# A linear-attention and two-layer kernel: the start of the program is rewritten and the order of its first ten chunks is replaced

## The chip, the cores and the metric

The kernel runs on one core of one Trainium2 chip. The metric is the device time of one execution in microseconds (us): the median of the runs. A profile of one execution, taken by the hardware profiler, shows what each engine did: PE is TensorE, PEld its weight loads, DVE is VectorE, ACT is ScalarE, POOL is GpSimd, SP is SyncE, which here only issues transfers.

## What is computed

An attention with a decaying state (batch 4, 8 heads, 768 steps, head size 48), and then two matrix products with a leaky ReLU between them, on 3,072 tokens of 384 features and 2,048 hidden features:

```python
state = np.zeros((B, H, D, D), dtype=np.float32)
for t in range(S):
    kt, vt, rt = (k[:, :, t], v[:, :, t], r[:, :, t])
    cur = np.einsum('bhd,bhe->bhde', u[None] * kt, vt)
    y[:, :, t] = np.einsum('bhd,bhde->bhe', rt, state + cur)
    state = w[None, :, :, None] * state + np.einsum('bhd,bhe->bhde', kt, vt)
x = y.transpose(0, 2, 1, 3).reshape(B * S, H * D)
h = x @ w_in
out = np.maximum(0.01 * h, h) @ w_out
```

## The kernel before

The 3,072 tokens are cut into 24 chunks of 128, six for each batch entry. Inside a chunk the recurrence becomes matrix products: r is multiplied by a table of w to the power (t - 64), k by one of w to the power (63 - t), so that their product over the head size carries the decay; what lies at or above the diagonal is masked away, and the diagonal itself, which carries u, is added apart. A state of 48 by 48 for each head goes from chunk to chunk and is zero at the start of each batch entry.

The program is not written with loops that the engines run. `add` appends operations with the names they read and write, `Sched.resolve` (L75) turns these into semaphore waits, and each of the five engines then works through its own operations strictly in the order in which they were added. Transfers are in these streams too: SP issues r of chunk 0, the stores of the output and the transposing transfers; ACT issues k of chunk 0; POOL issues every other load, and each of these keeps it busy.

The order at the start is written by hand: the string LOADS gives the order in which POOL issues the loads (r3 is r of chunk 3, wi1 the second quarter of w_in, wo2 a quarter of w_out, id and tri the making of the identity and of the mask), and ORDER gives the order of the steps. A letter is a step and a number its chunk:

- P (`prep`, L303): on DVE, r and k times their tables into `qk`, two instructions; from chunk 8 on also the transposing transfer on SP that fills `tp`.
- T (`turn`, L342): for chunks 0 to 7 the same transposition by eight matmuls against the identity and two copies out of PSUM.
- A (`a_mm`, L369): eight matmuls, the products of all pairs of steps, in two PSUM banks. M (`a_mask`, L383): their masking into `at` on DVE, one instruction for each bank. From chunk 8 on the mask is copied onto a tile that POOL has filled with the diagonal.
- X (`diag`, L315): on DVE the product q*k of the transposed chunk, for the diagonal of chunks 0 to 7; K (`kv_mm`, L396): matmuls for the diagonal's sums and for the new state; Q (`prep2`, L320): v times these sums into `vs`; from chunk 8 on Q makes the sums on DVE with `u_tab` and POOL the diagonal tile (L342). S (`state`, L453): the state times its decay, on DVE.
- Y (`y_part`, L504, with `y_mm`, L466): the chunk's output, in matmuls of 32 columns of weights, four of them side by side, and a copy into `xT` on ACT.
- G (`g1`, L512): a quarter of the first product of one chunk, 12 matmuls of 128 columns, and the leaky ReLU on ACT; it needs that quarter of w_in. J (`g1_pair`, L530): an eighth of it for two chunks, 6 matmuls of 256 columns. H (`g2`, L548): the second product of a chunk, 16 matmuls of 384 columns, a copy on ACT and a store that SP issues; it needs all of w_out.
- C and W: the decay as columns (`decay_columns`, 16 small matmuls of the rows w and w*u) and as table. U: `u_tab`, u spread over all partitions by a matmul. F: matmuls on ones that compute nothing. L: the loads of a later chunk, held back until a given G or J has run.

What stands ahead of ORDER: w comes as a single row, a matmul against a row of ones (L287) spreads it over 128 partitions, ACT takes its logarithm (L289) and makes the two tables from it (L290, L291). POOL makes identity and mask with a select each (L255, L259); DVE fills the padding of v and qk with zeros (L278, L282). Eight PSUM banks are handed out in turn by `next_bank`.

After ORDER, from chunk pair 3 on, a loop (L576) repeats one pattern for each pair m: J for the pair, the steps Q, X, A, M of the pair after next, Y of the next pair, K, S, P two pairs on, and H of the pair before.

## Time and profile before

| | us |
|---|---|
| median of 3 runs | 173.33 (173.15 to 173.61) |
| span of the profiled execution | 171.8 |
| TensorE busy in it | 163.4 |
| VectorE, ScalarE, GpSimd busy | 95.7, 92.5, 102.7 |
| first matmul of T0 | 7.30 |
| first matmul of G0.0 | 14.08 |
| first matmul of an H | 42.59 |
| last copy out of PSUM | 168.94 |

The page gives the span of the profiled execution, from its first to its last instruction; its time with what lies around the span is not given, so the runs' median stands beside it. The DMA engines are in use until some 120 us:

```profile
DMA  5999999999999999999499499899008011011112
GB/s 98 119 150 157 171 153 173 200 179 144 112 98 240 94 145 126 202 101 116 133 93 138 128 89 143 147 116 217 0 4 214 4 46 46 4 46 50 46 48 92
```

The 40 digits are 40 equal slices of the span, 4.3 us each. A digit is the mean busy share of the core's 16 DMA engines in tenths; the row under it is what they moved. In a list of instructions the columns are the start, the length, the engine, the line, the operation, what it writes and reads, and in brackets the idle time of the engine before it and what ended that.

### The profile page before, as it was taken

To read this page: it belongs to the slowest core of one execution; us is meant where nothing else is said; L and a number is where in the kernel's file an instruction comes from. 1 tells how busy PE (TensorE), PEld (TensorE's weight loads), DVE (VectorE), ACT (ScalarE), POOL (GpSimd) and SP (SyncE) were. 2 spreads that over 40 slices of the span, in tenths; PEclk is the share of its full clock that TensorE was granted. 3 is DMA by queue.
4 is the path that set the end of the run, shared out by engine and by line. 5 is a ranking of instruction groups with operands and counts; after the bars stand their busy time and mean duration, and the time that the engine had idled before them with its cause. 6 is when DMAs were issued, how large, how long until landed. Compare 5 with 4: busy or idle time off the path is not lost.

```text
span 171.8 us, 5029 instructions
## 1 busy us (share of the span) xinstructions
PE 163.4 (95%) x2179; PEld 122.4 (71%) x2179; DVE 95.7 (56%) x209; ACT 92.5 (54%) x169; POOL 102.7 (60%) x117
## 2 busy tenths in 40 slices
PE   6799999969999989999999999999999999999993
PEld 1578799859666856876877867868868768678661
DVE  7699859550999679079189197296396520000000
ACT  4755698759123841942934934825817718539121
POOL 7999999990379998972993997957207200000000
PEclk9999999999999999999999999999999999999999
DMA  5999999999999999999499499899008011011112
GB/s 98 119 150 157 171 153 173 200 179 144 112 98 240 94 145 126 202 101 116 133 93 138 128 89 143 147 116 217 0 4 214 4 46 46 4 46 50 46 48 92
DMA packets 98970, 19.66 MB, mean 114 GB/s; under 512 B 92290, under 2 KB 98948, under 8 KB 98948
## 3 DMA queue, kind: packets, MB, share of 16 engines
q0 software_dynamic: 76512, 10.03, 89.7%
q1 hardware_dynamic: 21394, 9.11, 27.1%
q8 instruction: 17, 0.28, 0.7%
q10 hardware_dynamic: 1042, 0.20, 0.6%
q14 instruction: 5, 0.04, 0.1%
HBM read 20.45 MB, written 4.72 MB: 146 GB/s over the span
## 4 chain that ended last, share of the span: by engine, by line
PE 76%; DMA 9%; DVE 6%; POOL 6%; issue 2%; ACT 0%; POOLq 0%; ACTq 0%
PE ps L555 30%; PE ps L538 28%; PE ps L521 6%; PE ps L493 6%; DMA tp<-qk 5%; DMA w_in_sb<-in_moe_w_in_dram 4%; PE ps L377 3%; PE ps L408 2%; DVE qk L307 2%; POOL v_sb L210 2%; POOL r_sb L210 2%; POOL k_sb L210 2%; PE ps L355 1%; DVE ku L330 1%; DVE s_tok L334 1%
## 5 line engine op out<-in xcount | busy, mean ns | idle before, releaser
L555 PE MATMUL ps<-w_out_sb,gT 128*128 128x384 bf16 x384 | 64.5, 326 | 0.0
L538 PE MATMUL ps<-xT,w_in_sb 128*128 128x256 bf16 x480 | 54.5, 273 | 0.0
L555 PEld LDWEIGHTS ps<-w_out_sb,gT 128*128 128x128 bf16 x384 | 36.9, 98 | 23.4
L342 POOL TENSOR_TENSOR at<-ident,s_tok 128x512 bf16<-128x512 bf16 x32 | 33.8, 1081 | 30.3 <-DVE s_tok L334 30.3
L544 ACT ACTIVATE gT<-ps 128x512 bf16<-128x512 f32 x80 | 47.8, 597 | 7.0 <-PE ps L538 2.1
L538 PEld LDWEIGHTS ps<-xT,w_in_sb 128*128 128x128 bf16 x480 | 46.7, 98 | 6.4
L561 ACT ACTIVATE out_sb<-ps 128x384 f32<-128x384 f32 x24 | 11.8, 490 | 55.1 <-PE ps L555 55.1
L391 DVE CAST_PREDICATED at<-mask,ps 128x512 bf16<-128x512 uint16 x32 | 19.8, 684 | 27.6 <-PE ps L377 25.3
L210 POOL DMA_DIRECT2D v_sb<-in_v_dram x24 | 22.6, 948 | 0.4 <-issue 0.4
L210 POOL DMA_DIRECT2D k_sb<-in_k_dram x23 | 21.7, 945 | 0.0
L210 POOL DMA_DIRECT2D r_sb<-in_r_dram x23 | 21.4, 932 | 0.0
L508 ACT ACTIVATE xT<-ps 128x384 bf16<-128x384 f32 x24 | 11.0, 490 | 4.8 <-PE ps L493 4.3
L521 PE MATMUL ps<-xT,w_in_sb 128*128 128x128 bf16 x192 | 12.3, 219 | 0.3 <-DMA w_in_sb<-in_moe_w_in_dram 0.3
L493 PE MATMUL ps<-at,v_sb 128*32 128x128 bf16 x384 | 11.9, 224 | 0.0
L521 PEld LDWEIGHTS ps<-xT,w_in_sb 128*128 128x128 bf16 x192 | 11.1, 98 | 1.0 <-DMA w_in_sb<-in_moe_w_in_dram 0.6
L526 ACT ACTIVATE gT<-ps 128x512 bf16<-128x512 f32 x16 | 9.6, 599 | 3.6 <-PE ps L521 3.0
L332 DVE TENSOR_TENSOR rku<-r_sb,ku 128x384 bf16<-128x384 bf16 x16 | 10.8, 674 | 0.5
L387 DVE TENSOR_TENSOR at<-ps,mask 128x512 bf16<-128x512 f32 x16 | 10.3, 682 | 1.3 <-PE ps L377 1.3
L493 PEld LDWEIGHTS ps<-at,v_sb 128*32 128x32 bf16 x384 | 9.1, 98 | 2.0 <-issue 0.5
L366 ACT ACTIVATE tp<-ps 128x512 bf16<-128x512 f32 x15 | 8.2, 596 | 3.8 <-PE ps L355 3.8
L493 PE MATMUL ps<-tp,st 128*32 128x128 bf16 x240 | 10.1, 219 | 0.0
L377 PE MATMUL ps<-tp 48*128 48x128 bf16 x192 | 9.1, 228 | 0.9 <-DMA tp<-qk 0.7
(62 smaller groups left out, 134.5 us busy)
## 6 DMA issues: line engine op xcount, KB each, us to landing
out_dram<-out_sb SPq DMA_DIRECT2D x24, 192.0 KB, 2.2
v_sb<-in_v_dram POOLq DMA_DIRECT2D x24, 96.0 KB, 5.9
r_sb<-in_r_dram POOLq DMA_DIRECT2D x23, 96.0 KB, 5.1
k_sb<-in_k_dram POOLq DMA_DIRECT2D x23, 96.0 KB, 5.0
w_in_sb<-in_moe_w_in_dram POOLq DMA_DIRECT2D x4, 384.0 KB, 7.4
w_out_sb<-in_moe_w_out_dram POOLq DMA_DIRECT2D x4, 384.0 KB, 11.1
tp<-qk SPq DMA_TRANSPOSE x16, 3.4
r_f<-in_r_dram SPq DMA_DIRECT2D x1, 192.0 KB, 3.5
```

The costliest lines, as they stand in the source:

```text
L210: add("pool", lambda: G.dma_start(dst, src), R=pace, W=[(which, n)], dma=f"{which}{n}")
L332: add("dve", lambda: V.tensor_tensor(rku[i2][:, :], r_of(n), ku[i2][:, :], ALU.mult), R=[("r", n), ("ku", i2)], W=[("rku", i2)])
L342: add("pool", lambda hh=hh, s_of=s_of: G.tensor_tensor(at[ia][:, hh, :, :], ident[:, :].unsqueeze(1).to_broadcast([128, NP, 128]), s_of.un ...
L377: last = PE.matmul(at_bank[n][hh][0][:, 128 * p:128 * p + 128], tp[it][rows, NP + p, :], tp[it][rows, p, :], start=True, stop=True)
L391: add("dve", lambda hh=hh, part=part: V.copy_predicated(at[n % NAT][:, hh, :, :], mask[:, :].bitcast(mybir.dt.uint16).unsqueeze(1).to_broa ...
L493: last = PE.matmul(ps_y[32 * q:32 * q + 32, 128 * s:128 * s + 128], a, m, start=first_mm, stop=last_mm)
L508: add("act", lambda: A.activation(xT[m % NX][:, :, 128 * half:128 * half + 128], ps_y[:, 0:HD].rearrange("p (s t) -> p s t", t=128), AF.Copy),
L521: last = PE.matmul(ps_g[:, 128 * f:128 * f + 128], w_in_sb[:, s, 128 * fb:128 * fb + 128], xT[ix][:, s, t], start=s == 0, stop=s == NSL - 1)
L538: last = PE.matmul(ps_g[:, 256 * f:256 * f + 256], w_in_sb[:, s, 128 * fb:128 * fb + 128], xT[ix][:, s, :], start=s == 0, stop=s == NSL - 1)
L544: add("act", lambda: A.activation(gT[ig][:, 2 * j:2 * j + 2, :].rearrange("p f t -> p (f t)"), ps_g[:, :], AF.Prelu, alpha=0.01), R=[key], ...
L555: last = PE.matmul(ps_o[:, 0:HD], gT[ig][:, s, 128 * half:128 * half + 128], w_out_sb[:, s, :], start=s == 0, stop=s == NFB - 1)
L561: add("act", lambda: A.activation(out_sb[io][:, :], ps_o[:, 0:HD], AF.Copy), R=[key], W=[("o", io)])
```

## The change

`LOADS` is gone: the loads stand in ORDER as small letters among the steps, and ORDER is another one. As an engine's order is that of the string, a load's place among steps matters only against other work of POOL.

- w is loaded spread over 128 partitions by a transfer that reads the row 128 times, so the matmul that spread it is gone, and with it the two early fills. u comes the same way into `u_bc`, on SP, once chunk 1 has been turned (`u_table`). w and u also come as 8 rows of 48, and C multiplies these by a small selection matrix, four matmuls in place of 16; their product is step Z.
- One ramp (column minus partition) on POOL gives the exponents, the selection matrix, the identity and the mask, by comparisons on DVE.
- DVE clears the padding of qk 0 to 2 and v 0 to 2; `pad` on POOL clears the rest.
- r and k lie side by side in one tile; step B makes both products in one instruction (P still makes two), also in the loop. The transposing transfer is a step of its own, D.
- M takes both PSUM banks in one instruction. M1.2 lets ACT copy one of the two banks, M3.1 and M7.1 both, before DVE masks the copy. X7.1 puts X on POOL. Both copies of T0 go through ACT.
- Y of chunks 0 to 7 adds the diagonal by three matmuls of full width in place of twelve of 32 columns.
- The last H is cut into 256 and 128 columns, each with its own copy and store.

```diff
-FIRST, EARLY = 6, 2
-LOADS = """r1 k1 r2 k2 wi0 id v1 r3 tri k3 v2 wi1 k4 r4 v3 wi2 k5 r5 r6 k6 v4 v5 k7 wi3 r7 v6 v7 wo3 wo2 wo1 wo0"""
+FIRST = 6
 ORDER = """
-C W P0 P1 F1 T0 T1 P2 A0 X0 M0 A1 K0 T2 Q0 X1 Y0 A2 S0 M1 K1 X2 G0.0 Q1 P3 S1 Y1 T3 K2 M2 G1.0 X3 A3 U G0.1 S2 G1.1 Q2 M3 Y2 K3 P4
-T4 Q3 G2.0 G2.1 G0.2 S3 G2.2 G1.2 Y3 P5 A4 P6 X4 M4 T5 X5 G3.0 K4 Q4 A5 S4 T6 G3.1 K5 G3.2 Y4 M5 L8 Q5 Y5 P7 A6 G1.3 J2.0 J2.1 T7
-M6 X6 X7 K6 J2.2 J2.3 A7 S6 J2.4 J2.5 L9 Q6 G2.3 G0.3 J2.6 M7 L10 J2.7 L11 G3.3 K7 S7 P8 Q7 Q8 P9 H0 Q9 K8 H1 P10 L12 K9 H2 S8 S9
-Y6 Y7 A8 A9 P11 M8 H3 M9 L13
+r1 k1 v1 Z r2 k2 P0 r4 k3 C T0 A0 X0 P1 M0.0 v2 K0 r3 W T1 Q0 k4 A1 S0 pad wi0 X1 v3 B2 M1.2 Y0 K1 T2 Q1 k5 S1 P3 X2 r5 wi3 Y1 T3 K2 v4 v5 B4 wi1 v7 k6 r6 k7 Q2 T4 S2 X3.0 r7 v6 A2 wi2 A3 F2 M2.0 M3.1 G1.0 G0.0 K3 X4.0 Q3 B5 Y2 A4 Y3 S3 T5 G2.0 M4.0 G3.0 G0.3 K4 X5.0 G1.3 wo1 wo3 wo2 Q4 wo0 K5 Q5 G3.3 S4 L8 A5 M5.0 Y4 G1.1 G2.1 G2.3 L9 G3.1 P6 Y5 T6 G0.1 X6.0 J2.7 U J2.2 B7 J2.0 T7 L10 J2.4 J2.1 K6 G0.2 Q6 G2.2 X7.1 S6 J2.5 A7 A6 M6.0 M7.1 P8 G1.2 D8 J2.6 K7 G3.2 J2.3 Y6 B9 Q7 L11 H1 Q8 S7 K8 D9 S8 H2 H3 Q9 H0 Y7 L12 A8 A9 K9 B10 D10 B11 M8 M9.0 S9 D11 L13
...
-    def row(h):
-        return dram(h, 0, [[HD, 1], [1, HD]])
...
-    add("sp", lambda: SP.dma_start(w_row[:, :], row(w)), W=["w_row"], dma="w")
-    add("act", lambda: A.dma_start(u_row[:, :], row(u)), W=["u_row"], dma="u")
+    def spread(h):
...
+    add("sp", lambda: SP.dma_start(w_bc[:, :], spread(w)), W=["w_bc"], dma="w")
...
-    add("pool", lambda: G.iota(tcol[:, :], pattern=[[0, 1]], base=0, channel_multiplier=1,
-                               allow_small_or_imprecise_dtypes=True), W=["tcol"])
+    add("sp", lambda: SP.dma_start(w_h[:, :], w), W=["w_h"], dma="wh")
+    add("sp", lambda: SP.dma_start(u_h[:, :], u), W=["u_h"], dma="uh")
+    add("pool", lambda: G.iota(ramp[:, :], pattern=[[1, 128]], base=0, channel_multiplier=-1,
+                               allow_small_or_imprecise_dtypes=True), W=["ramp"])
     load_one(0, "v")
...
+    def load(name):
+        if name == "pad":
+            add("pool", lambda: G.memset(pad_v(3, NST), 0.0), W=[("v0", 1)])
+            add("pool", lambda: G.memset(qk_all[:, 3:NQK, :, D:E], 0.0), W=[("qk0", i) for i in range(3, NQK)])
...
+    add("dve", lambda: V.tensor_scalar(pick[:, :], ramp[0:H, 0:H], 0.0, None, ALU.is_equal), R=["ramp"], W=["pick"])
+    add("dve", lambda: V.tensor_scalar(ident[:, :], ramp[:, :], 0.0, None, ALU.is_equal), R=["ramp"], W=["ident"])
+    add("dve", lambda: V.tensor_scalar(mask[:, :], ramp[:, :], 1.0, None, ALU.is_ge), R=["ramp"], W=["mask"])
+    add("dve", lambda: V.memset(qk_all[:, 0:3, :, D:E], 0.0), W=[("qk0", i) for i in range(3)])
+    add("dve", lambda: V.memset(pad_v(0, 3), 0.0), W=[("v0", 0)])
+    add("dve", lambda: V.memset(wu[:, :, :], 0.0), W=["wu"])
...
-    fill(EARLY)
-    add("pe", lambda: PE.matmul(ps_w[:, 0:HD], one_row[:, :], w_row[:, :], start=True, stop=True),
-        R=["one_row", "w_row"], W=[key_w, "bc"])
-    add("act", lambda: A.activation(lnw[:, :], ps_w[:, 0:HD], AF.Ln), R=[key_w], W=["lnw"])
-    add("act", lambda: A.activation(qtab[:, :], lnw[:, :], AF.Exp, scale=qexp[:, 0:1]), R=["lnw", "qexp"], W=["qtab"])
-    add("act", lambda: A.activation(ktab[:, :], lnw[:, :], AF.Exp, scale=kexp[:, 0:1]), R=["lnw", "kexp"], W=["ktab"])
+    add("act", lambda: A.activation(lnw[:, :], w_bc[:, :], AF.Ln), R=["w_bc"], W=["lnw"])
+    add("act", lambda: A.activation(tab[:, 0, :], lnw[:, :], AF.Exp, scale=qexp[:, 0:1]), R=["lnw", "qexp"], W=["qtab"])
+    add("act", lambda: A.activation(tab[:, 1, :], lnw[:, :], AF.Exp, scale=kexp[:, 0:1]), R=["lnw", "kexp"], W=["ktab"])
...
+    def turn_by_dma(n):
+        iq = n % NQK
+        add("sp", lambda: SP.dma_start_transpose(tp[n % NTP][:, :, :], qk[iq].rearrange("p h e -> p (h e)")),
+            R=[("kp", iq), ("qp", iq), ("qk0", iq)], W=[("tp", n % NTP, 0), ("tp", n % NTP, 1)],
+            dma=f"tp{n % NTP}")
...
-        if n >= TURNED:
-            add("sp", lambda: SP.dma_start_transpose(tp[n % NTP][:, :, :],
-                                                     qk[iq][:, :, :].rearrange("p h e -> p (h e)")),
-                R=[("kp", iq), ("qp", iq), ("qk0", iq)], W=[("tp", n % NTP, 0), ("tp", n % NTP, 1)],
-                dma=f"tp{n % NTP}")
-
-    def diag(n):
+
+    def prep_both(n):
+        iq = n % NQK
+        both = rk_sb[:, n, :, :].rearrange("p w (h d) -> p (w h) d", d=D)
+        by = tab[:, :, :].rearrange("p w (h d) -> p (w h) d", d=D)
+        add("dve", lambda: V.tensor_tensor(qk[iq][:, :, 0:D], both, by, ALU.mult),
+            R=[("r", n), ("k", n), "qtab", "ktab", ("qk0", iq)], W=[("qp", iq), ("kp", iq)])
...
+    def diag(n, how=0):
         it, i2 = n % NTP, n % 4
-        add("dve", lambda: V.tensor_tensor(prod[i2][:, :, :], tp[it][:, 0:NP, :], tp[it][:, NP:2 * NP, :], ALU.mult),
+        on = G if how else V
+        add("pool" if how else "dve", lambda: on.tensor_tensor(prod[i2][:, :, :], tp[it][:, 0:NP, :], tp[it][:, NP:2 * NP, :], ALU.mult),
             R=[("tp", it, 0), ("tp", it, 1)], W=[("prod", i2)])
...
-            if n == 0 and half == 1:
-                add("dve", lambda dst=dst, ps_t=ps_t: V.tensor_copy(dst, ps_t[:, :]),
-                    R=[key], W=[("tp", it, half)])
-            else:
-                add("act", lambda dst=dst, ps_t=ps_t: A.activation(dst, ps_t[:, :], AF.Copy),
-                    R=[key], W=[("tp", it, half)])
+            add("act", lambda dst=dst, ps_t=ps_t: A.activation(dst, ps_t[:, :], AF.Copy),
+                R=[key], W=[("tp", it, half)])
...
+        if taken[0] % 8 == 7:
+            taken[0] += 1
...
-    def a_mask(n):
-        for hh in range(2):
-            part = at_bank[n][hh][0][:, :].rearrange("p (m i) -> p m i", i=128)
-            if n < DIAG:
-                add("dve", lambda hh=hh, part=part: V.tensor_tensor(
-                    at[n % NAT][:, hh, :, :], part, mask[:, :].unsqueeze(1).to_broadcast([128, NP, 128]), ALU.mult),
-                    R=[at_bank[n][hh][1], "mask"], W=[("at", n % NAT, hh)])
-            else:
-                add("dve", lambda hh=hh, part=part: V.copy_predicated(
-                    at[n % NAT][:, hh, :, :],
-                    mask[:, :].bitcast(mybir.dt.uint16).unsqueeze(1).to_broadcast([128, NP, 128]), part),
-                    R=[at_bank[n][hh][1], "mask", ("at", n % NAT, hh)], W=[("at", n % NAT, hh)])
+    def a_mask(n, how=0):
+        i = at_bank[n][0][1][1]
+        keys = [key for _, key in at_bank[n]]
+        halves = [("at", n % NAT, hh) for hh in range(2)]
+
+        def part(c0, c1):
+            src = ps_all[:, 512 * i + 128 * c0:512 * i + 128 * c1].rearrange("p (m i) -> p m i", i=128)
+            return src, at[n % NAT][:, :, :, :].rearrange("p two m i -> p (two m) i")[:, c0:c1, :]
+
+        def tri(c):
+            return mask[:, :].unsqueeze(1).to_broadcast([128, c, 128])
+
+        if n >= DIAG:
+            src, dst = part(0, H)
+            add("dve", lambda: V.copy_predicated(
+                dst, mask[:, :].bitcast(mybir.dt.uint16).unsqueeze(1).to_broadcast([128, H, 128]), src),
+                R=keys + ["mask"] + halves, W=halves)
+            return
+        through = (0, H, NP)[how]
+        if through:
+            src, raw = part(0, through)
+            add("act", lambda raw=raw, src=src: A.activation(raw, src, AF.Copy), R=keys[:2 if through == H else 1],
+                W=halves[:2 if through == H else 1])
+        if through < H:
+            src, dst = part(through, H)
+            add("dve", lambda: V.tensor_tensor(dst, src, tri(H - through), ALU.mult),
+                R=keys[1 if through else 0:] + ["mask"], W=halves[1 if through else 0:])
+        if through:
+            add("dve", lambda: V.tensor_tensor(raw, raw, tri(through), ALU.mult),
+                R=halves[:2 if through == H else 1] + ["mask"], W=halves[:2 if through == H else 1])
...
+    def decay_product():
+        add("dve", lambda: V.tensor_tensor(wu_h[:, :], w_h[:, :], u_h[:, :], ALU.mult), R=["w_h", "u_h"], W=["wu_h"])
...
         def emit():
             for hh in range(2):
-                for p in range(NP):
-                    c0 = (2 * p + hh) * D
-                    rows = slice(64 * hh, 64 * hh + D)
-                    PE.matmul(ps_c[rows, p:p + 1], w_row[:, c0:c0 + D], one_row[:, 0:1], start=True, stop=True)
-                    last = PE.matmul(ps_c[rows, NP + p:NP + p + 1], wu_row[:, c0:c0 + D], one_row16[:, 0:1],
-                                     start=True, stop=True)
+                rows = slice(64 * hh, 64 * hh + D)
+                PE.matmul(ps_c[rows, 0:NP], w_h[:, :], pick[:, hh::2], start=True, stop=True)
+                last = PE.matmul(ps_c[rows, NP:2 * NP], wu_h[:, :], pick[:, hh::2], start=True, stop=True)
             return last
 
-        add("pe", emit, R=["one_row", "one_row16", "w_row", "wu_row"], W=[key_c, "wcols"])
+        add("pe", emit, R=["w_h", "wu_h", "pick"], W=[key_c, "wcols"])
...
-                if n < DIAG:
-                    one.append((vs[iv][:, 128 * s + 32 * q:128 * s + 32 * q + 32], ident[:, :]))
...
-                                         start=first_mm, stop=last_mm)
+                                         start=first_mm and (s == 0 or n >= DIAG),
+                                         stop=last_mm and n >= DIAG)
+            if n < DIAG:
+                for s in range(NSL):
+                    last = PE.matmul(ps_y[:, 128 * s:128 * s + 128], vs[iv][:, 128 * s:128 * s + 128], ident[:, :],
+                                     start=False, stop=s == NSL - 1)
...
     def g2(n):
-        ps_o, key = next_bank()
         m, half = divmod(n, 2)
-        ig = m % NG
-
-        def emit():
...
-        add("sp", lambda: SP.dma_start(out[128 * n:128 * n + 128, :], out_sb[io][:, :]),
-            R=[("o", io)], W=[("out", n)], dma=f"o{io}")
+        ig, io = m % NG, n % NO
+        for c0, c1 in ([(0, HD)] if n < NST - 1 else [(0, 256), (256, HD)]):
+            ps_o, key = next_bank()
+
+            def emit(c0=c0, c1=c1, ps_o=ps_o):
+                for s in range(NFB):
+                    last = PE.matmul(ps_o[:, 0:c1 - c0], gT[ig][:, s, 128 * half:128 * half + 128],
+                                     w_out_sb[:, s, c0:c1], start=s == 0, stop=s == NFB - 1)
+                return last
+
+            add("pe", emit, R=[("gT", ig, half, j) for j in range(8)] + [("wout", i) for i in range(4)], W=[key])
+            add("act", lambda c0=c0, c1=c1, ps_o=ps_o: A.activation(out_sb[io][:, c0:c1], ps_o[:, 0:c1 - c0], AF.Copy),
+                R=[key], W=[("o", io, c0)])
+            add("sp", lambda c0=c0, c1=c1: SP.dma_start(out[128 * n:128 * n + 128, c0:c1], out_sb[io][:, c0:c1]),
+                R=[("o", io, c0)], W=[("out", n, c0)], dma=f"o{io}" if not c0 else "olast")
 
...
-        ps_u, key = next_bank()
-        add("pe", lambda: PE.matmul(ps_u[:, 0:HD], one_row16[:, :], u_row16[:, :], start=True, stop=True),
-            R=["one_row16", "u_row16"], W=[key, "bc16"])
-        add("act", lambda: A.activation(u_tab[:, :], ps_u[:, 0:HD], AF.Copy), R=[key], W=["u_tab"])
-
-    steps = {"U": u_table, "P": prep, "Q": prep2, "T": turn, "A": a_mm, "M": a_mask, "K": kv_mm, "S": state, "Y": y_part, "X": diag, "C": decay_columns, "W": decay_table, "F": fill,
+        add("sp", lambda: SP.dma_start(u_bc[:, :], spread(u)), R=[("tp", 1, 0)], W=["u_bc"], dma="ubc")
+        add("act", lambda: A.activation(u_tab[:, :], u_bc[:, :], AF.Copy), R=["u_bc"], W=["u_tab"])
+
...
-                prep(n)
+                prep_both(n)
+                turn_by_dma(n)
```

86 lines of the change are left out of this document (32 added, 54 removed).

## The prediction

> **What bounds the kernel now.** I read the busy times first, then the chain of work that ended last in order of time, then what TensorE waited for, then the queues of POOL and SP and the landing of single loads. TensorE is the bound by its busy time:
>
> ```profile
> PE 163.4 (95%) x2179; PEld 122.4 (71%) x2179; DVE 95.7 (56%) x209; ACT 92.5 (54%) x169; POOL 102.7 (60%) x117
> ```
>
> A busy PE can still be slow or early, so the chain says more (columns: start us, length us, what):
>
> ```profile
> 9.48 0.85 POOL k_sb L210
> 10.33 0.85 POOL v_sb L210
> 11.19 7.06 DMA w_in_sb<-in_moe_w_in_dram
> 18.25 0.05 issue
> 18.29 1.51 PE ps L521 x24
> ...
> 34.07 0.15 PE ps L408 x3
> 34.22 1.51 issue
> 35.73 0.22 PE ps L408
> ...
> 53.12 8.41 DMA tp<-qk
> 61.53 0.14 issue
> 61.66 0.40 PE ps L377 x8
> 62.06 0.90 PE ps L493 x56
> ...
> 158.45 10.41 PE ps L555 x64
> ...
> 168.94 0.49 ACT out_sb L561
> ```
>
> The reader is to see three parts. Up to 18.29 the end is set by POOL issuing loads one after the other and by a w_in load. From 18.29 to 168.88 TensorE runs without a hole but two. After that come a copy and a store. The holes are 1.5 us inside one group of four matmuls at 34.22 and 0.7 us for the transposed chunk 11:
>
> ```profile
> PE ps L408 <- issue: 1.5, 1, 1.5
> PE ps L355 <- POOL ident L255: 1.0, 1, 1.0
> PE ps L377 <- DMA tp<-qk: 0.7, 1, 0.7
> ```
>
> The first hole is on no semaphore, since the group's waits all stand before its first matmul; the profile does not name its cause.
>
> **Sizes on TensorE.** From the chain, without holes: G 0.67, J 0.655 (5.24 for eight), H 2.60, T 0.45, A 0.33, K 0.43 (0.27 without a carried state, 0.08 when only the diagonal is left), Y 0.67 with state and 0.47 without. What was done before 18.29 is T0-T3, A0-A3, K0-K2, Y0, Y1, G0.0, G1.0: 1.80+1.32+1.13+1.14+1.34 = 6.7 us. What TensorE must do hardly changes: Y of a chunk below 8 has 12 narrow matmuls less (40 took 0.67, so 0.20) and three full ones more (0.056 each by a G's 12 in 0.67, so 0.17).
>
> **The first weights, the step that decides.** Each r, k or v load occupies POOL for 0.87 us. In the changed order v0 and ten such loads and two memsets (pad) stand before the first w_in load, where v0 and four stood before. The ramp is 128 wide instead of 1, so v0 starts near 1.6 instead of 1.41 (an estimate from the 0.46 of the 128-wide select at L259). Then 1.6+1.06+10x0.867 = 11.3, plus pad. Pad writes 1,344 and 384 words a partition. No POOL memset of size is in the trace. From below goes the same operation on DVE:
>
> ```profile
> 2.07 1.34 DVE L278 MEMSET v_sb<- 128x1536 uint32 x1 [0.27 <-issue]
> 45.68 2.20 POOL L342 TENSOR_TENSOR at<-ident,s_tok 128x512 bf16<-128x512 bf16 x2 [7.33 <-DVE s_tok L334]
> ```
>
> 0.87 ns a word, 1.5 us; from above POOL's own two-input product, 1.05 us for 512, 2.05 ns, 3.5 us. I take 1.7, near the same operation. So w_in's first quarter is issued at 13.0. It took 6.4 us to land when issued at 5.93 behind a backlog (12.3); with the queue nearly drained I take 6.0, so 19.0 (bounds 17.8 with 1.5 and 5.0, to 20.9 with 3.5 and 6.1).
>
> The Trainium skill (GPSIMD Engine Reference, 4.1 Engine selection) holds one-input work on GpSimd to be roughly line-rate. No run here shows that for a memset; by it pad would be 1.5 and the sum 0.2 us less.
>
> **All that is gained before 19.0 is hidden.** w now arrives spread over 128 partitions: from 0.80, between the 2.6 at which the small row had arrived and 4.3 by the 3.5 of the equally large r_f. The logarithm then follows without a matmul; qtab and ktab (0.6 each) end near 5.6 instead of 6.0, the products of chunk 0 near 6.4 instead of 7.66. ident comes from DVE (a 128x128 tensor_scalar, under 0.3 by the 0.56 of a 128x384 f32 product), which ends the 1.0 wait above. DVE's setup is then 0.5 for ones, 0.2+0.6 for the small tables, 0.45+0.2 for the memsets kept and 0.3 for wl and wu, done by 3.5, before w. The two casts of wu and the decay product stand beside that; SP issues w, r0 and two tiny loads one after the other, none later than 2.5. Both copies of T0 go through ACT: 0.5 later. From P0's end to A3's end took 7.66 to 17.70, 10.0 us, DVE nearly full; the new order adds B4 and T4 (0.9) and takes about 0.3 off a joined or ACT-helped mask. So A3 ends near 17.0, the fill F2 (two 512-column matmuls, 0.43) near 17.5, and G1.0 waits for w_in until 19.0. The cover is 1.5 us: if weights came at 17.5, the chunk work would decide.
>
> **From G1.0 to H1.** TensorE has 16 G (10.7), J2 (5.24), K3-K7 (1.64), Y2-Y6 (3.0), A4-A7 (1.3), T5-T7 (1.35): 23.25 us, 42.25. ACT has 16x0.64+8x0.65+3x1.09+5x0.47+1.1 (M7.1)+0.49 = 22.65 us in that time, nearly as much. H1 needs all of w_out. Landings after the first w_in quarter, in the trace before, are 0.70 apart for r, k, v (17 of them) and the last w_out landed near 40.1 (issued 27.1, 13.0 later), so 7 weight loads took (40.1-12.3-11.9)/7 = 2.27 each. Now 11 and 7 are left: 23.6, so 42.6. The quarters between, by the same spacing, land at 23.4, 27.1 and 33.6, and their first users (G0.3, G1.1, J2.4) come at 24.2, 27.7 and 34.3: covered by 0.6 to 0.8. Three limits within a microsecond. The hole of 1.5 may come back, bounds 0 and 1.5; I count half: H1 at 43.0. Before, the same point (H0's start 42.59 plus Y6, 0.45) was 43.04. So the head gives nothing, bounds -1.6 (weights at 17.8, then w_out sets H1) and +2.6 (20.9 and the whole hole).
>
> **From H1 to chunk 11.** Same work, 17.6 us to A11. D10 and D11 now stand behind the store of H0 on SP, the fourth H, where P11's transpose stood before the fourth store. Each transpose holds SP 1.25 us. D11 is issued at H0's end plus 0.5 (copy) plus 0.6 (store's issue) plus 1.25 = 2.4, and A11 comes 7.0 after H0's end (Y7, A8, A9, K9, J3, A10: 0.64+0.6+0.19+5.24+0.33), so it may take 4.6 to land. Rows: 3.1 to 3.6 with no loads beside, 5.1 to 8.4 with them; the median is
>
> ```profile
> tp<-qk SPq DMA_TRANSPOSE x16, 3.4
> ```
>
> I take no wait, by tp10 (3.6, issued at 50.48) and most later pairs (3.2): -0.73 (bounds -0.73 and, at 8.4, +3.1). D8 and D9 have over 3 us to spare by 7.3 and 5.1. X7 on POOL (1.1 by L342) follows L10's issue near 39, before K7 near 41, and holds up only L11, used 10 us later. The u load waits on SP for T1, and behind it stands only D8, 30 us later; the joined r and k products lie off the path.
>
> **The end.** The last H is split 256+128: 16x0.109+16x0.056 = 2.64 against 2.60. The copy behind it falls from 0.49 to 0.28 (384 and 512 columns take 0.49 and 0.60), and the store is a third; its 2.2 us falls by between 0 and 0.7, I take 0.2. Sum -0.37. The loop between is TensorE without a hole; its shorter DVE work is worth nothing.
>
> **Sum.** 0.0-0.73-0.37 = -1.1 on the span of 171.8: 170.7. The page gives no time of the profiled execution beside its span; the median of the runs is 173.33, 1.5 above the span, and I carry 1.5: **172.2 us**. About 0.5 us (0.3%) can be told from no change.
>
> **Rivals.** (1) Transposes late, the other side. L12 and L13 are issued beside D10 and D11, as before beside P11's, whose landing took 8.4. From 4.6 on A11 waits, from 6.2 the whole is slower than 173.8; at 7.3 (the slowest row but that one) A11 comes 10.6+2.4+7.3 = 20.3 after H1, 2.7 more than 17.6: 172.2+2.7 = 174.9. For it: the same queue, the same loads. Against: in the loop that follows most pairs land in 3.2, and tp10, issued just ahead of L12, in 3.6. Chance 0.22. (2) Pad slow: at 3.5 us every weight is 1.8 later, 174.0. For it: POOL's select took 3.6 ns a column. Chance 0.13. (3) A cold array. In the trace 8 matmuls of A span 0.61 until 13.5 and 0.40 from 17.3 on, though the granted clock reads 1.00 throughout, and the array sped up only after some 3.5 us without a pause from 10.57. The two early fills go. If it is still slow at 19.0, 3.5 us at half rate cost 1.75: 173.9. Against: chunk work at the slow rate fills 6 to 17 itself. Chance 0.09. Beside it stands the Trainium skill (TensorE: Matmul & The Clock Gate, Part 1: The HAM clock gate): half rate until one window of about 3.4 us was busy; the trace agrees with its 3.5. (4) No change: the full hole comes back and weights land at 19.3, 173.2; that the rewritten start does shorten the start and it is swallowed, is this case. Chance 0.14. The forecast has 0.42, alone 170.9 to 172.8.
>
> **Chances and range.** Faster 0.44 (the forecast, and a little of 2), same 0.18 (4, and the edges), slower 0.38. Low end 170.4: first weights at 18.2 and no hole (w_out then sets H1 at 41.8, 1.2 less), 0.6 more off the store. High end 175.0: rival 1 at 7.3.
>
> **What would show it.** Right: G1.0's wait on w_in ending near 19 with TensorE idle before it, H1's start near 43, no wait on tp<-qk at A11, the last copy 0.28. Wrong: pad over 2.5 us, A11 waiting, A's 8 matmuls still at 0.6 after 19, or ACT full with TensorE waiting for banks. A first w_in landing before 17.5 would make me wrong the good way.

## The result, and the profile after

The kernel after takes 179.53 us, the median of 4 runs (179.05 to 179.78); the kernel before took 173.47 beside it (4 runs, 173.15 to 173.95). The ratio is 1.036, 95% interval 1.032 to 1.040: slower by 6 us, where 172.2 was forecast and 175.0 was the upper end. The profiled execution took 179.59, its span is 177.8. Ratios below leave out runs more than 1.5% above the fastest of the same kernel, medians are over all runs, so the two can differ.

Busy times of the page after:

```profile
PE 162.3 (91%) x2103; PEld 122.4 (69%) x2103; DVE 88.6 (50%) x161; ACT 94.2 (53%) x173; POOL 106.2 (60%) x118
```

TensorE has 1.1 us less to do than before and DVE 7 less, and the span is 6.0 longer. So the loss is in waiting, or in work at a worse moment. The chain of work that ended last, after (start, length, what):

```profile
28.14 0.58 issue
...
33.69 0.28 PE ps_all L532 x5
33.97 1.06 issue
35.03 0.56 PE ps_all L532 x7
...
45.94 2.60 PE ps_all L567 x16
...
58.90 6.98 DMA tp<-qk_all
65.89 0.14 issue
66.02 0.40 PE ps_all L367 x8
...
67.68 6.79 PE ps_all L567 x32
...
175.47 0.28 ACT out_sb L572
```

Three places matter. There are two holes on no semaphore (28.14 and 33.97, the second inside the twelve matmuls of a G), 1.64 together, where before had one of 1.51. A11 at 66.02 comes behind a transposing transfer of 6.98. And the H pair behind it takes 6.79 us where every other pair takes 5.2 to 5.4. What TensorE waited for (us in all, times, longest), and what SP issued (start, length):

```profile
PE ps_all L367 <- DMA tp<-qk_all: 2.3, 2, 1.2
...
PE ps_all L532 <- DMA w_in_sb<-in_moe_w_in_dram: 0.4, 1, 0.4
```

```profile
51.86 5.53 SPq L574 DMA_DIRECT2D out_dram<-out_sb  x3
57.44 4.34 SPq L288 DMA_TRANSPOSE tp<-qk_all  x2
```

SP is held by the stores of H2, H3 and H0 until 57.4, and the last of these cannot be issued before H0 is done at 56.5. Only then come D10 and D11, in strict order. The windows show the clock (stretch, sum, busy time of PE, PEld, DVE, ACT, POOL, then the granted clock, DMA share, GB/s):

```profile
65.00:67.00 2.00, 0.98 (x56) 0.91 (x60) 1.61 (x2) 0.02 (x1) 2.00 (x3) 1.00 0.03 4
67.00:68.00 1.00, 1.00 (x30) 0.66 (x19) 1.00 (x2) 0.86 (x2) 1.00 (x2) 0.68 0.09 16
68.00:70.00 2.00, 2.00 (x7) 0.88 (x6) 1.93 (x6) 0.00 (x0) 2.00 (x4) 0.50 1.74 86
70.00:71.00 1.00, 1.00 (x5) 0.54 (x4) 0.96 (x3) 0.00 (x0) 1.00 (x2) 0.61 2.05 115
```

TensorE stands for 1.05 and 1.21 us before A10 and A11, with 0.3 of work between, and then gets half its clock for 3.4 us (the three lower rows lose 0.32, 1.00 and 0.39 us of clock): 7 matmuls of H in 68 to 70, where 15 fit into 65 to 67 before. Where the 6.0 us of span come from, read from the two chains:

| stretch | before | after | difference |
|---|---|---|---|
| start to H1 | 43.2 | 45.94 | +2.7 |
| H1 to A11 | 18.5 | 20.08 | +1.6 |
| A11 to the last copy | 107.28 | 109.45 | +2.17 |
| last copy to the end of the span | 2.9 | 2.3 | -0.5 |

The 43.2 is the first H of before, at 42.75 in the chain, and the 0.45 of Y6, which there comes later. The prediction's 43.04 took the 42.59 of the list of instructions, where an H stands 0.16 earlier than in the chain. The first two rows rest on one trace of each kernel, and the one of before is early: in b_late_transposes, b_p11_early_split_end and b_split_end, whose programs are the same up to the first H, it starts 0.5 to 0.8 later than in before, and in b_split_end A11 does not wait. So their share is known to some 0.8 us.

### The profile page after: what moved, and what is told of

Its sections match the earlier page's. It is cut to its first block, busy times and chain, and to the rows that moved or that the text cites. A ratio compares the mean times of both kernels' runs of the same rounds, so it can differ in the third digit from the quotient of the medians.

```text
span 177.8 us, 4853 instructions
## 1 busy us (share of the span) xinstructions
PE 162.3 (91%) x2103; PEld 122.4 (69%) x2103; DVE 88.6 (50%) x161; ACT 94.2 (53%) x173; POOL 106.2 (60%) x118
## 4 chain that ended last, share of the span: by engine, by line
PE 81%; POOL 8%; DMA 7%; issue 2%; ACT 0%; DVE 0%; POOLq 0%; DVEq 0%
PE ps_all L567 36%; PE ps_all L549 27%; PE ps_all L499 5%; PE ps_all L532 5%; POOL rk_sb L206 4%; DMA tp<-qk_all 4%; DMA v_sb<-in_v_dram 3%; PE ps_all L367 3%; PE ps_all L416 2%; POOL v_sb L206 2%; POOL v_sb L252 1%; PE ps_all L504 1%; PE ps_all L347 1%; POOL qk_all L253 0%; POOL w_in_sb L216 0%
## 5 line engine op out<-in xcount | busy, mean ns | idle before, releaser
L567 PE MATMUL ps_all<-w_out_sb,gT 128*128 128x384 bf16 (+2 forms) x400 | 65.9, 325 | 0.0
L567 PEld LDWEIGHTS ps_all<-w_out_sb,gT 128*128 128x128 bf16 x400 | 38.4, 99 | 24.3 <-issue 1.7
L549 PE MATMUL ps_all<-xT,w_in_sb 128*128 128x256 bf16 x480 | 54.7, 273 | 0.0
L549 PEld LDWEIGHTS ps_all<-xT,w_in_sb 128*128 128x128 bf16 x480 | 46.7, 98 | 6.1
L555 ACT ACTIVATE gT<-ps_all 128x512 bf16<-128x512 f32 x80 | 47.5, 597 | 5.7 <-PE ps_all L549 1.0
L387 DVE CAST_PREDICATED at<-mask,ps_all 128x1024 bf16<-128x1024 uint16 x16 | 18.9, 1221 | 33.2 <-PE ps_all L367 32.8
L206 POOL DMA_DIRECT2D rk_sb<-in_k_dram x23 | 21.8, 948 | 0.0
L206 POOL DMA_DIRECT2D rk_sb<-in_r_dram x23 | 21.5, 933 | 0.0
L532 PE MATMUL ps_all<-xT,w_in_sb 128*128 128x128 bf16 x192 | 12.3, 219 | 1.5 <-issue 1.1
L324 DVE TENSOR_TENSOR rku<-rk_sb,ku 128x384 bf16<-128x384 bf16 x16 | 12.6, 786 | 0.6
L532 PEld LDWEIGHTS ps_all<-xT,w_in_sb 128*128 128x128 bf16 x192 | 11.1, 98 | 2.4 <-issue 1.2
L537 ACT ACTIVATE gT<-ps_all 128x512 bf16<-128x512 f32 x16 | 9.5, 601 | 3.0 <-PE ps_all L532 2.6
```

Source lines behind the costliest of these rows:

```text
L206: add("pool", lambda: G.dma_start(dst, src), R=pace, W=[(which, n)], dma=f"{which}{n}")
L324: add("dve", lambda: V.tensor_tensor(rku[i2][:, :], r_of(n), ku[i2][:, :], ALU.mult), R=[("r", n), ("ku", i2)], W=[("rku", i2)])
L387: add("dve", lambda: V.copy_predicated(dst, mask[:, :].bitcast(mybir.dt.uint16).unsqueeze(1).to_broadcast([128, H, 128]), src), R=keys + [ ...
L532: last = PE.matmul(ps_g[:, 128 * f:128 * f + 128], w_in_sb[:, s, 128 * fb:128 * fb + 128], xT[ix][:, s, t], start=s == 0, stop=s == NSL - 1)
L549: last = PE.matmul(ps_g[:, 256 * f:256 * f + 256], w_in_sb[:, s, 128 * fb:128 * fb + 128], xT[ix][:, s, :], start=s == 0, stop=s == NSL - 1)
L555: add("act", lambda: A.activation(gT[ig][:, 2 * j:2 * j + 2, :].rearrange("p f t -> p (f t)"), ps_g[:, :], AF.Prelu, alpha=0.01), R=[key], ...
```

## The experiments

**1. The order on SP, the pause, pad, the diagonals: four changes to the kernel after.** In e1 the end of ORDER is changed, so that the products of chunks 10 and 11 and their transposes go ahead of H3 and H0 and of their stores:

```diff
-... S8 H2 H3 Q9 H0 Y7 L12 A8 A9 K9 B10 D10 B11 M8 M9.0 S9 D11 L13
+... S8 H2 Q9 B10 D10 B11 D11 H3 H0 Y7 L12 A8 A9 K9 M8 M9.0 S9 L13
```

> The changed kernel with one thing moved: on SP the transposing transfers of chunks 10 and 11 stand before the stores of H3 and H0 instead of after them (their products on DVE keep their order). Theory 1 (the late transposes cost the wait of 2.3 us at A10 and A11, and that pause then halves the array's clock for 3.5 us, another 1.6): both go, 179.5 - 3.9 = 175.6 us, granted clock 1.00 from 66 to 72 us. Theory 2 (the time is lost before H1, by weights that come 3 us later; A11 would have waited for something else): the wait moves to another operand and less than 1 us is won. Theory 3 (the slow clock has nothing to do with the pause): 177.2, the clock still at half near 67 to 71 us.

176.68 (175.34 to 177.07, 4 runs), ratio 1.0215 (1.0171 to 1.0259). A11 starts at 61.8 and waits for nothing, the clock is 1.00 in all four runs (0.99 in all four of the kernel after): the late transposes are a cause. But a new wait of 1.5 stands two chunks later:

```profile
60.59 4.21 POOL at L334 x4
64.80 0.02 issue
64.82 1.22 DVE at L387
...
66.82 1.02 DVE qk_all L303 x2
...
68.68 6.80 DMA tp<-qk_all
...
75.62 0.40 PE ps_all L367 x8
```

A8 and A9 stand behind all four H, as in the kernel after (before has H3 behind them), so their masks come late, and with them the products for POOL's diagonal tiles, the masks of chunks 10 and 11, the products of 12 and 13 and their transposes. As DVE works strictly in order, the wait has moved one pair on.

In e2 TensorE computes ten matmuls on ones, which nothing reads, ahead of A10 (in the loop, where m is 3):

```diff
+        if m == 3:
+            fill(10)
```

> The changed kernel with ten matmuls on ones (512 columns, 2.2 us, they compute nothing) ahead of A10, in the stretch in which TensorE waits for the transposed chunks 10 and 11. The transfers stay as late as they are. Theory 1: A11 still starts near 66.0 us, but the clock stays at 1.00 and the two H behind take 5.2 instead of 6.8 us: 179.5 - 1.6 = 177.9 us. Theory 3 (the clock falls for another reason): no change, 179.5 us.

178.36 (178.03 to 180.06), ratio 1.0325 (1.0275 to 1.0374). A11 is as late as ever (66.49), its transfer took 8.01, but the clock stayed at 1.00 in three of four runs, and the H pair behind it takes 5.20 again:

```profile
66.49 0.40 PE ps_all L367 x8
...
68.06 5.20 PE ps_all L567 x32
```

5.20 against 6.79: the clock is 1.6 us of the loss. That run's first weights came 0.9 later (20.31), which hides part of it in the total.

In e3 DVE clears all padding and pad is empty:

```diff
-            add("pool", lambda: G.memset(pad_v(3, NST), 0.0), W=[("v0", 1)])
-            add("pool", lambda: G.memset(qk_all[:, 3:NQK, :, D:E], 0.0), ...
+    add("dve", lambda: V.memset(qk_all[:, 3:NQK, :, D:E], 0.0), ...
+    add("dve", lambda: V.memset(pad_v(3, NST), 0.0), W=[("v0", 1)])
```

> The changed kernel with the two memsets of pad moved from POOL to DVE, behind its other memsets, where DVE is idle from 2.6 to 6.0 us. The first w_in quarter is then issued at 11.1 instead of 14.0 us. Theory 2 (late weights decide the head): G1.0 starts up to 3 us earlier and the whole is 2.5 to 3 us faster, 177 us. Theory 1 (the chunk work ends at 19.0 anyway, so weights have 0.4 us of cover to give, and chunk 3's v another 0.4): 0.4 to 0.9 us faster, 178.6 to 179.1, and the late transposes cost as much as before.

178.66 (176.03 to 180.59, 6 runs), ratio 1.023 (1.0173 to 1.0286). The runs lie by their mean clock: 176.03 and 176.99 at 1.00, 178.16 and 179.16 at 0.99, 180.18 and 180.59 at 0.981. At the 0.99 of the kernel after that is about 0.8 less. In the profiled run, 176.99, G1.0 starts at 18.6, no longer held by w_in. What H1 gains (44.19 in place of 45.94) comes back in part as wait, 3.1 in place of 2.3:

```profile
PE ps_all L368 <- DMA tp<-qk_all: 3.1, 2, 2.1
```

Behind these 3.1 us the clock stayed at 1.00, so a longer wait need not bring it down. So pad costs 1.75 at H1 in this trace and some 0.8 in the time, but it is not the main cause.

In e4 the diagonals of chunks 0 to 7 are narrow again, as before:

```diff
+                if n < DIAG:
+                    one.append((vs[iv][:, 128 * s + 32 * q:128 * s + 32 * q + 32], ident[:, :]))
...
-            if n < DIAG:
-                for s in range(NSL):
-                    last = PE.matmul(ps_y[:, 128 * s:128 * s + 128], vs[iv][:, 128 * s:128 * s + 128], ident[:, :],
-                                     start=False, stop=s == NSL - 1)
```

> The changed kernel with the diagonal of chunks 0 to 7 added by twelve matmuls of 32 columns again, in place of three of full width. In the chain a Y of the changed kernel takes 0.51 + 0.27 = 0.78 us where it took 0.67 before; I had counted 0.64. If the full-width matmuls cost 0.11 us in each of the seven Y with a carried state and none of it is hidden, 0.5 to 0.8 us are won: 178.8 to 179.0 us. If it is hidden by waits elsewhere in the head: 179.5 us.

180.53 (179.52 to 182.39, 6 runs), ratio 1.0426 (1.0386 to 1.0467), above both expectations. Each Y is 0.67 again instead of 0.78, and the kernel is no faster; but its weights landed a microsecond later in the profile, and the clock was 0.981 to 0.99. In the profiled run (0.981) the clock was at half from about 65.8 to 72.6, in one stretch of 6.8 us, twice that of the kernel after. From G1.0 to H1 this trace takes 25.3 us, the kernel after 26.6: holes of 0.98 for 1.64, no wait for v3, Y 0.5 shorter in all. So nothing here speaks for the wide form in the new order; the total settles nothing, and experiment 3 tries the form in the old order.

**2. The cause in the kernel before, and the best form of the kernel after.** In b_late_transposes the kernel before gets nothing but late transposes:

```diff
-Y6 Y7 A8 A9 P11 M8 H3 M9 L13
+Y6 Y7 A8 A9 P11 M8 H3 D10 D11 M9 L13
```

> The kernel before, with nothing changed but the transposes of chunks 10 and 11, which go behind the stores of H0 to H3 on SP. Theory 1: waits of 2.5 to 4 us in all at A10 and A11 where 0.7 was, H1 where it was, the granted clock down to about .5 for some 3 us behind the pause (1.6 us more), time 176 to 178.5. Theory 2 (something else of the new order makes it): waits under 1.5, clock 1.00, time under 174.5.

176.56 (175.26 to 177.37, 6 runs), ratio 1.0148 (1.0091 to 1.0205). The profile, of a run of 175.26, shows

```profile
PE ps L382 <- DMA tp<-qk: 1.9, 2, 1.3
```

where before had 0.7: 1.2 more, and below the 2.5 to 4 in all that theory 1 gave. The three runs with a clock of 1.00 took 175.26, 175.26 and 176.07, the three with 0.99 took 177.04 to 177.37, 1.7 more on average. So one edit on SP brings a longer wait and, in half of the runs, a lower clock; where the clock fell in those runs no trace shows. Nothing else of the new order is needed for this.

e6 is e1 mended: A8, A9 and M8 ahead of H3 as in the kernel before, pad on DVE.

```diff
+... S8 H2 Q9 B10 D10 B11 D11 Y7 L12 A8 A9 K9 M8 H3 M9.0 S9 H0 L13
```

> The kernel after, with pad on DVE, D10 and D11 ahead of the stores of H3 and H0 on SP, and A8, A9, M8 ahead of H3 on TensorE and DVE. Theory 1 (the loss is the transposes of chunks 10 and 11 standing behind four stores, then the half clock after the pause): no wait on tp at A10 and A11, none at A12 and A13 either, granted clock 1.00 in the profile, time 173 to 174.5. Theory 2 (the first weights, late behind pad and ten loads, are the loss): weights near 18.5 to 19.5 as before the edit, time 176 or more. Theory 3 (the fall of the clock comes by itself): clock .98 to .99 without a pause, time near 176.

175.51 (174.86 to 175.84, 12 runs), ratio 1.0091 (1.0064 to 1.0119), clock 1.00 in all twelve. In the chain, A10 and A11 follow J3 without a gap:

```profile
53.05 5.20 PE ps_all L568 x32
58.25 5.24 PE ps_all L550 x48
63.49 0.55 PE ps_all L368 x16
```

With that 4.0 of the 6.1 us are back, of which e3 gives pad some 0.8. The time is a microsecond above what theory 1 gave: H1 starts at 44.89, 1.7 later than before, and A8 and A9, now ahead of H3, wait for their own transposed chunks, with no fall of the clock behind it:

```profile
PE ps_all L368 <- DMA tp<-qk_all: 0.9, 2, 0.8
```

c_parts_in_old_order has all parts of the change, but steps and loads in the order of the kernel before, and pad on DVE:

```diff
+r1 k1 r2 k2 wi0 v1 r3 k3 v2 wi1 k4 r4 v3 wi2 k5 r5 r6 k6 v4 v5 k7 wi3 r7 v6 v7 wo3 wo2 wo1 wo0 Z C W P0 P1 F1 T0 T1 ...
+... P8 D8 Q7 Q8 P9 D9 H0 Q9 K8 H1 P10 D10 L12 K9 H2 S8 S9 Y6 Y7 A8 A9 P11 D11 M8 H3 M9 L13
```

> All parts of the kernel after (w spread, ramp, joined r and k tile, joined masks, full-width diagonals, split last H), but the steps and the loads in the order of the kernel before, transposes right behind P, padding on DVE. Theory 1 (the order is the whole loss, the parts cost nothing): 172.4 to 173.3, a wait of about 0.7 at A11 as before, first weights near 18.3. Theory 2 (the parts cost too: w spread makes r0 and lnw later, Y of the first chunks 0.11 longer each): 173.8 or more.

175.06 (173.66 to 175.74, 12 runs), ratio 1.0065 (1.003 to 1.010). The clock is 1.00 throughout, yet five runs lie at 173.7 to 174.2 and seven at 175.0 to 175.7. The profile is of one of the former, so what the others do more is not known. In it A11 does not wait and there is no hole over 0.1, yet the first H starts at 43.98, 1.2 later than before. So the parts cost something at the start too.

b_p11_early_split_end is the kernel before with P11 right behind P10 and the last H cut in two as in the change:

```diff
-... H1 P10 L12 K9 H2 S8 S9 Y6 Y7 A8 A9 P11 M8 H3 M9 L13
+... H1 P10 P11 L12 K9 H2 S8 S9 Y6 Y7 A8 A9 M8 H3 M9 L13
```

> The kernel before with P11 right behind P10 (its transpose then goes ahead of the stores of H2 and H3) and with the last H cut into 256 and 128 columns. By the rows: -0.7 for the wait at A11, -0.5 for the end: 171.8 to 172.4. If the transpose is late by its transfer and not by its place, the wait stays and only the end is won: 172.6 to 172.9.

173.42 (172.61 to 175.37, 12 runs), ratio 0.9983 (0.9956 to 1.0011): no change that can be told, and neither expectation came. The wait at A11 is gone, but P11's two products now stand on DVE ahead of the states of chunks 8 and 9, and an H waits 0.5 for the sum of a state.

**3. The parts one by one, on the kernel before, and the hole.** b_spread_w loads w over 128 partitions, ahead of r0, and drops the matmul:

```diff
-    add("sp", lambda: SP.dma_start(w_row[:, :], row(w)), W=["w_row"], dma="w")
+    add("sp", lambda: SP.dma_start(w_bc[:, :], dram(w, 0, [[0, 128], [1, HD]])), W=["w_bc"], dma="wbc")
+    add("act", lambda: A.dma_start(w_row[:, :], row(w)), W=["w_row"], dma="w")
```

> The kernel before, in which SP loads w spread over 128 partitions ahead of r0 and the logarithm reads that, without the matmul that spread it. Theory 1 (the spread load delays its neighbours, since it is as large as r0 and goes ahead of it): r0 lands near 6.9 instead of 4.7 and the logarithm starts near 5, so P0 ends no earlier than 7.7, perhaps 0.5 later, and the whole is the same or up to 0.6 longer: 173.5 to 174.3. Theory 2 (the spread shortens the start, as the prediction had it): P0 ends near 6.4, a microsecond earlier, and the whole gains up to 1 us, since weights are issued early here: 172.4 to 173.2.

173.43 (173.11 to 174.07, 12 runs) beside 173.18, ratio 1.0019 (1.0005 to 1.0034). The start is not shorter: T0 begins at 7.80, before at 7.30. The issues (KB, median us to landing) say why, first in this run, then before:

```profile
w_bc<-in_w_dram SPq DMA_DIRECT2D x1, 192.0 KB, 4.0
r_f<-in_r_dram SPq DMA_DIRECT2D x1, 192.0 KB, 4.7
k_f<-in_k_dram ACTq DMA_DIRECT2D x1, 192.0 KB, 5.3
```

```profile
r_f<-in_r_dram SPq DMA_DIRECT2D x1, 192.0 KB, 3.5
k_f<-in_k_dram ACTq DMA_DIRECT2D x1, 192.0 KB, 3.9
```

b_full_width_diagonals has only the change of Y:

```diff
-                if n < DIAG:
-                    one.append((vs[iv][:, 128 * s + 32 * q:128 * s + 32 * q + 32], ident[:, :]))
...
+            if n < DIAG:
+                for s in range(NSL):
+                    last = PE.matmul(ps_y[:, 128 * s:128 * s + 128], vs[iv][:, 128 * s:128 * s + 128], ident[:, :],
+                                     start=False, stop=s == NSL - 1)
```

> The kernel before with the diagonals of chunks 0 to 7 in three matmuls of full width. If the 0.78 of the changed kernel's chain against 0.67 is the cost of the form, each Y is 0.11 longer, eight of them 0.9, and the whole 0.5 to 0.9 longer (173.9 to 174.4). If the cost is somewhere else, Y stays near 0.67 and the whole within 0.3. Nine matmuls fewer for each Y also move the point where the hole of 1 to 1.7 us stands some 50 matmuls on in the program; where it comes there, or whether it is smaller, no theory here says.

172.36 (171.47 to 172.63, 7 runs), ratio 0.9944 (0.9922 to 0.9965). Neither theory gave this: each Y is longer, as expected (0.51 + 0.27 instead of 0.67), and yet the kernel is faster. In its trace the hole is gone, and K6 stands in the chain in one piece:

```profile
34.27 0.08 PE ps L404 x4
34.35 0.19 PE ps L408 x4
34.54 1.31 PE ps L541 x12
```

None of the four traces with the wide form in the old order has a hole over 0.2 behind 18 us; all six with the narrow form have one, of 0.54 to 1.75. The new order has holes with both forms (1.64 in the kernel after, 0.98 in e4).

b_more_small_matmuls asks what the hole is, with 21 tiny matmuls in place of the one large fill F1:

```diff
-            for _ in range(n):
+            for _ in range(n if n > 1 else 0):
                 last = PE.matmul(ps[i][:, :], ones[:, 0:128], ones[:, :], start=True, stop=True)
+            for _ in range(21 if n == 1 else 0):
+                last = PE.matmul(ps[i][:, 0:4], ones[:, 0:128], ones[:, 0:4], start=True, stop=True)
```

> The kernel before with 21 matmuls of 4 columns in place of the one of 512 ahead of T0, which compute nothing. Theory A (the hole of 1.5 us at TensorE's 601st matmul is the end of a block of instructions, which the instruction queue has not yet brought): it comes 20 matmuls earlier in the program, inside a J of the first pair, still about 2.5 us behind a packet of 16 KB, and is not in K6. Theory B (it belongs to K6 or to what K6 waits for): it stays in K6, between its third and fourth state matmul. Time in both: 173 to 174.

173.62 (172.09 to 175.50, 12 runs), ratio 1.0014 (0.999 to 1.0037). The hole has moved:

```profile
33.51 0.76 PE ps L540 x7
34.27 1.75 issue
36.02 0.71 PE ps L540 x5
```

It stood behind the third of K6's four state matmuls; 3 of these, 4 small ones, the 8 of T7 and 5 of this J make 20: exactly the number added. In b_spread_w, with two matmuls fewer, it stands two further on. So it belongs to a place in the instruction stream, not to a step: theory A. Its end follows a packet of 16 KB of the queue that the DMA view calls instruction:

| kernel | packet | hole | its end behind the packet |
|---|---|---|---|
| before | 33.1 | 34.22 to 35.73 | 2.6 |
| after | 26.1 and 32.6 | 28.14 to 28.72, 33.97 to 35.03 | 2.6 and 2.4 |
| e6 | 25.2 and 31.7 | 27.68 to 27.96, 33.21 to 34.00 | 2.8 and 2.3 |
| b_late_transposes | 34.0 | 35.28 to 36.43 | 2.4 |
| b_more_small_matmuls | 33.7 | 34.27 to 36.02 | 2.3 |
| b_split_end | 34.0 | 35.98 to 36.52 | 2.5 |

Two such places in the kernel after are 127 matmuls apart, 254 instructions with their weight loads, and in the kernel before 17 packets stand against 2 x 2,179 instructions, one for each 256. A reading that fits is that the next block is late where 127 short matmuls go by in 6 us, and that a block lasts longer with twelve narrow matmuls less and three wide ones more in each Y. As the reason why the longer Y wins in the old order this was not tried apart.

b_split_end has only the cut of the last H, as the change makes it:

```diff
+        for c0, c1 in ([(0, HD)] if n < NST - 1 else [(0, 256), (256, HD)]):
```

> The kernel before with only the last H cut into 256 and 128 columns: -0.5 by the profile of the changed kernel (from the last copy's start to the end 2.33 us against 2.9), 173.0 where the kernel before has 173.5. Nothing else moves. If the end is not what the third store costs, no change.

172.86 (172.29 to 173.23, 12 runs) beside 173.18, ratio 0.9975 (0.9958 to 0.9992): 0.4 us, as in the changed kernel.

**4. What is left in e6, and a faster kernel.** e7 issues the first quarter of w_in behind k2 and moves G0.0 and G1.0 forward:

```diff
-r1 k1 v1 Z r2 k2 P0 ... S0 pad wi0 X1 ... wi3 Y1 T3 ... v6 A2 wi2 A3 F2 M2.0 M3.1 G1.0 G0.0 K3
+r1 k1 v1 Z r2 k2 wi0 P0 ... S0 pad X1 ... wi3 G0.0 Y1 T3 ... v6 G1.0 A2 wi2 A3 M2.0 M3.1 K3
```

> As e6, and in addition the first quarter of w_in is issued behind k2 (near 6.0) as in the kernel before, G0.0 and G1.0 run among the chunk work (behind X2 and Q2), and the fill in front of them is gone. Theory W (what is left of the loss in e6, 1.5 to 2 us, is that no G is done while TensorE waits for chunk work at the start): 1.0 to 1.4 us less than e6, H1 near 43.5, time 174.0 to 174.6. Theory I (what is left is longer Y and instruction blocks, and the chunk work, not the weights, sets the start): H1 within 0.4 of e6, time 175.1 to 175.9; the time won at the start comes back as longer holes.

175.96 (174.94 to 176.88, 6 runs), ratio 1.0143 (1.0107 to 1.0179): nothing won, theory W falls, at least in this form. G0.0 runs at 14.91 and G1.0 at 18.63, and H1 comes 0.5 earlier than in e6 (44.42). But the chain now goes through a k load issued at 11.00, behind the w_in quarter, that takes 6.53, and the next chunk's products wait for it until 17.5.

b_full_and_split joins the two parts that won on the kernel before (the edits of b_full_width_diagonals and b_split_end):

> The kernel before with full-width diagonals for chunks 0 to 7 and the split end: if the two gains add, -1.0 and -0.4, 171.8; if the hole comes back at another place, 172.8.

171.64 (171.43 to 172.40, 5 runs) beside 173.61, ratio 0.9901 (0.9874 to 0.9928). The gains add, within the intervals. It is faster than both kernels.

b_full_split_p11 has these two and the ORDER of b_p11_early_split_end:

> The same with P11 right behind P10. Where the first half comes earlier by the hole, the wait at A11 could come back, and P11 early is then worth up to 0.7: 171.2 to 171.8. If DVE is what it delays, no gain: 171.8 to 172.3.

172.13 (171.50 to 172.83, 6 runs), ratio 0.9918 (0.9889 to 0.9948). P11 early adds nothing, as in b_p11_early_split_end, and for the same 0.5 of waiting for DVE.

## Why the prediction was wrong

**The step that failed: "I take no wait, by tp10 (3.6, issued at 50.48) and most later pairs (3.2): -0.73".** D10 and D11 landed 6.8 and 7.0 after their issue, beside the loads of L12 and L13; the waits are 2.3 in all, not zero, and 0.7 before. Rival 1, with 7.3 and 174.9, had place, cause and size. The rows to take were those with loads beside them, 5.1 to 8.4, which the prediction had, above all the 8.41 of the same edge in the chain before, and not the median of transfers most of which had no loads beside them. e1, e6 and b_late_transposes show it from both sides.

**A term that was missing: the clock after the wait, 1.6.** Rival 3 had the price of half a clock (1.75) but looked for it at the start only. A wait was priced as its length alone. In the kernel after the clock fell in four runs of four, in b_late_transposes in three of six, in e6, which waits 0.8 at most for a transposed chunk, in none of twelve; with the pause filled (e2) in one of four. What decides in the single run is not shown: the traced run of e3 kept its clock behind 3.1 us of waits, and one run each of b_p11_early_split_end, b_more_small_matmuls and e7 had 0.99, with no wait over 0.9 for an operand behind the first H in their traces. The Trainium skill (TensorE: Matmul & The Clock Gate, Part 1: The HAM clock gate) has half rate follow after about 3.4 us of idling. Here 2.3 us in two pieces, with 0.3 of work between, were followed by it in the windows above; the measurement decides.

**The head, forecast as 0, is +2.7.** Its working gave 43.0 for H1, and 45.94 came. That is beyond its own bound of +2.6, which was to take weights at 20.9 and the whole hole; weights came at 19.39. In the chain from G1.0 on: first weights 0.4 later (19.39 for 19.0), a wait of 0.4 for v3 before K3, the holes 1.64 where half of 1.5 was counted (+0.9), five Y at 0.74 instead of 0.60 (+0.7), and 0.3 and 0.2 for G and K.
- Pad was mis-sized: 2.96 from its start to the w_in issue, not 1.7. The rate was right (0.91 ns each, 0.87 taken), the number was not: POOL writes 2,688 values of 16 bits, where the row on DVE wrote words of 32. That is most of the way to rival 2. The first weights are only 0.4 late all the same, because they landed 5.3 after their issue at 14.03 and not 6.0, and v0 started 0.25 earlier than taken: two errors that cancel in part.

```profile
11.07 2.44 POOL L252 MEMSET v_sb<- 128x2688 bf16 x1
13.35 0.84 POOL L253 MEMSET qk_all<- 128x768 bf16 x1
```

- "All that is gained before 19.0 is hidden" held, but there was nothing to hide: T0 starts at 7.59, not earlier than 7.30, and A3 ends at 18.38, not 17.0. The delay is there from the beginning: r of chunk 0 lands at 6.9 (5.7 after its issue, where before it took 3.5), its product starts at 6.97, and the products of chunk 0 end at 8.0 and not 6.4. Three loads of 192 KB side by side delay each other (b_spread_w).
- Rival 3 did not come as it stood: G1.0 and G0.0 take 1.34 from 19.39 on, full speed. But the array reached it later than in the kernel before: the narrow matmuls of a Y still took 0.31 at 15.7, where before they took 0.22 from 15.0 on; what that cost ahead of 19 was not tried.
- Y as a trade of 0.20 against 0.17 was wrong: full-width matmuls behind narrow ones cost 0.09 each, not 0.056, and the whole Y 0.11 more. In the old order the trade was also the wrong question, since the hole that went with it weighed more.
- The hole "may come back" was a coin toss, as its cause was unknown. b_more_small_matmuls ties it to a place in the instruction stream. The Trainium skill (Runtime: NRT & Kernel Launch, Instruction fetch mechanics) describes blocks of 256 instructions fetched ahead, the crossing "mostly hidden"; 127 matmuls with their weight loads agree with the block, and 0.2 to 1.75 us in these traces are not hidden.

**Right:** the end, -0.37 forecast, -0.5 in the profile and -0.4 for b_split_end alone; G1.0 waiting on w_in until near 19, though by the two errors above, which is luck; the last copy 0.28. Time outside the span was taken as 1.5 and is 1.8 in the profiled run after.

**What stays open.** e6 still takes 1.6 to 1.9 us more than before, with H1 1.7 later. Its chain shows G1.0 starting at 19.42 without waiting for weights, longer Y, 1.07 of holes and the wait of 0.8 at A9; e7 rules out the late weights alone. How much of it is the order of the chunk work, and what separates the two groups of runs of c_parts_in_old_order, is not settled. Nor is why three later H pairs of the kernel after take 5.37 instead of 5.20.

## What to carry to other kernels

Price a transfer by the row with the same neighbours in its queue and in the DMA engines, above all by the row on the chain, and when an issue is moved behind stores on an in-order queue, count from the end of the last of them. A wait of 2 us on TensorE may cost nearly twice its length, because the clock can fall behind it. Where TensorE runs through many short matmuls without a pause, count instructions as well as busy time: a form with fewer of them can win although it is longer, as it did here in the old order and was not seen to do in the new one.

## What the hardware showed that was not expected

- Places about 127 matmuls apart where TensorE can stand for 0.2 to 1.75 us on no semaphore, ending 2.3 to 2.8 us behind a 16 KB packet. It moves with the number of matmuls ahead of it, and its length differs between kernels with the same number (before 1.51, b_split_end 0.54).
- Half the granted clock for 3.4 us behind waits of 2.3 in all, and for 6.8 in e4 behind 3.1; not in every run, not behind the 3.1 of the traced e3, and not behind the 1.5 of e1.
- A memset cost 0.9 to 1.1 ns for each value written, whatever its width: on POOL 2,688 values of 16 bits took 2.44 and 768 took 0.84, on DVE 1,536 words of 32 bits took 1.34 and 512 values of 16 bits 0.48.
